# Reordering the end of the first attention step: transposes, copies on two engines, and a weight conversion in finer stages

## The chip, the cores and the metric

The kernel runs on one core of a Trainium2 chip. The metric is the device time of one execution in microseconds; the time before is 619.28 us, the median of three runs (618.98 to 620.67). The engines are named as in the profile: PE is TensorE (PEld its weight loads), DVE is VectorE, ACT is ScalarE, POOL is GpSimd, SP is SyncE, whose queue issues most of the transfers.

## What is computed

The reference is an attention block of the RWKV6 kind, followed by a gated feed-forward layer:

```
batch, n_heads, seq, head_dim = (4, 8, 768, 48)
for t in range(S):
    cur = np.einsum('bhd,bhe->bhde', u[None] * kt, vt)
    y[:, :, t] = np.einsum('bhd,bhde->bhe', rt, state + cur)
    state = wt[:, :, :, None] * state + np.einsum('bhd,bhe->bhde', kt, vt)
...
x = y as (B*S, H*D) = (3072, 384)
h = x @ w_in                       # 384 x 2048
sp = log(1 + exp(h))
out = (h * erf(sp)) @ w_out        # 2048 x 384
```

The two weight matrices arrive as float64; everything else is float32.

## The kernel before

**Steps.** The work is cut into 12 steps `s`. A step takes 128 positions of two batch entries with eight heads each, that is 256 rows of x. Six pairs of steps go through the sequence; steps 0 and 1 are the two halves of the batch at the first 128 positions, so they start from a state of zero. The order of instructions on every engine is written out by hand: inside `tc.manual_schedule` each engine runs its instructions in the order of the Python code, and what an instruction waits for follows from the tiles that it reads and writes.

**Attention of one step (`attend`, steps 0 to 4).** In-chunk products are built up over six levels. At each level TensorE multiplies r and k (`level_products`, L436) into a PSUM tile `pp`, VectorE multiplies half of r and k in place with products of the decays (`scale`, L252), and the products are taken over into `own` (L651 at level 1, a predicated copy at L448 for levels 2 to 5, ScalarE copies at L455 at level 6). Level 2 and later read what the scaling of the level below has written. The decay products `tot_sb` are made ahead on GpSimd (`prepare`, L304). After level 6 come:

1. `from_own(s, own, 1)`: half of own times v into the PSUM tile `y` (L470);
2. eight transposes of the scaled k into PSUM (L663) and the copy to `kT` on ScalarE (L667);
3. `state_part`: kT times v (L522), for both 64-position chunks `h`;
4. `from_own(s, own, 0)`: the other half;
5. `middle`, the state after the first chunk (two copies on VectorE, L692, in step 0), `faded` on GpSimd (L693), and the state for the next pair (`S_next`, L695);
6. `through_state`: r times the state into `y` (L496), then `y` is copied to SBUF as `xT` and `y3` (L503, L505, L506), and six small transfers bring rows of y3 into the free rows of xT (L510), three issued by SP and three by ScalarE.

`keep_busy` and `stay_warm` (L631) issue matmuls in step 0 and once in step 1 whose results nobody reads.

**Feed-forward.** `hidden` multiplies w_in with xT (L731), eight pieces of 12 matmuls a step, and `project` multiplies w_out with the gated result (L754). They run as pieces between the levels of later steps: `place(n)` is called after level n+1 and at the end, and issues conversion work (`convert_at`), activations and pieces. In step 1 one piece of step 0's hidden part runs at each place, so L731 waits for xT of step 0 and for the converted w_in.

**Conversion.** Each weight pair of slices (768 KB) is loaded as int32 words on SP (`load`, L194, three buffers `words`) and made float32 from its high and low words: ScalarE scales the high word into a PSUM tile (L207) and the low word into one of two `rest` buffers (L209); VectorE shifts (L216) and joins the sign (L219), writing w_in_sb or w_out_sb; GpSimd adds rest (L223). There are 16 such slices. `CONVERT[s][n]` lists what is issued at place n of step s: `l` a load, `s` both ScalarE operations, `j` the three operations that end a slice. Each letter keeps its own count. While slices are under way (`turns["converting"]`), the products of the attention use `pp0` alone, and the conversion uses `pp1`.

Of the kernel before, what the change touches and what calls it, by code (L numbers as in the profile page):

```python
# [11 lines left out]
FP32 = mybir.dt.float32  # L12
I32 = mybir.dt.int32
U32 = mybir.dt.uint32
AF = mybir.ActivationFunctionType
ALU = mybir.AluOpType

P = 128
EP = 64
HC = 64  # L20
NC = 2
NJ = 2
# [19 lines left out]
LOG = 6  # L42
# [18 lines left out]
def kernel(  # L61
# [14 lines left out]
    nc = tc.nc  # L76
# [51 lines left out]
    def products(shape):  # L128


        n = 0 if turns["converting"] else turns["next"]
        turns["next"] = 1 - n
        return ps_p.tile(shape, FP32, name=f"pp{n}")
# [46 lines left out]
    def convert(weights):  # L180

        held = {}

        def load(i):
            if i >= len(weights):
                return
            dst, src = weights[i]
            if src.dtype == FP32:  # L190
                nc.sync.dma_start(out=dst, in_=src)
                return
            words = wide.tile([P, 2, DM, 2], I32, name="words", bufs=3)
            nc.sync.dma_start(  # L194
                out=words[:].rearrange("p i n two -> p i (n two)"), in_=src.bitcast(I32)
            )
            held[i] = [words]

        def scale(i):
            if i in held:  # L200
                words = held[i][0]
                low, high = words[:, :, :, 0], words[:, :, :, 1]
                base = ps_p.tile([P, 2, NP * C], FP32, name="pp1")[:, :, :DM]
                rest = wide.tile([P, 2, DM], I32, name="rest", bufs=2)


                nc.scalar.mul(out=base, in_=high.bitcast(FP32), mul=2.0**-112)  # L207

                nc.scalar.mul(out=rest[:], in_=low.bitcast(U32), mul=2.0**-29)  # L209
                held[i] += [base.bitcast(I32), rest]  # L210

        def join(i):
            if i in held:
                words, bits, rest = held.pop(i)
                into = weights[i][0].bitcast(I32)
                nc.vector.tensor_scalar(  # L216
                    out=bits, in0=bits, scalar1=3, scalar2=None, op0=ALU.logical_shift_left
                )
                nc.vector.scalar_tensor_tensor(  # L219
                    out=into, in0=words[:, :, :, 1], scalar=-(1 << 31), in1=bits,  # L220
                    op0=ALU.bitwise_and, op1=ALU.bitwise_or,
                )
                nc.gpsimd.tensor_tensor(out=into, in0=into, in1=rest[:], op=ALU.add)  # L223

        done = {"l": 0, "s": 0, "j": 0}
        for _ in range(3):
            load(done["l"])
            done["l"] += 1
        while True:
            what = yield  # L230
            {"l": load, "s": scale, "j": join}[what](done[what])
            done[what] += 1
            if weights[0][1].dtype != FP32:
                turns["converting"] = 0 < done["s"] and done["j"] < len(weights)
                turns["next"] = 0

    def rows(e, n=D):
        return slice(e * EP, e * EP + n)
# [4 lines left out]

    ready = {}

    def scale(s, level):

        in_t, tots = loaded[s][0], ready[s][1]
        half, nb = 1 << (level - 1), JP * C >> level
        n = 1 if s > DIRECT and level == LOG else 2  # L250
        halves = view(in_t[:, 0:2], half, [[JP * C - half, n], [2 * half, nb], [1, half]])
        nc.vector.tensor_mul(  # L252
            halves, halves, view(tots[level - 1], 0, [[1, n], [2, nb], [0, half]])
        )

# [228 lines left out]
    def through_state(s, xT):  # L484

        c, in_t, _, _, S, _, _ = parts_of(s)
        for h, state in enumerate((S, middle)):
            if not (c or h):
                continue
            t = slice(h * HC, (h + 1) * HC)  # L490
            for j in range(NJ):
                for q in range(0, NP, 2):
                    for e in range(NE):
                        for p in (q + e, q + 1 - e):
                            n = j * NP + p
                            nc.tensor.matmul(  # L496
                                y[at(e, p), e, j, p // 2, t],
                                lhsT=state[rows(e), n, :], rhs=in_t[rows(e), 0, n, t],
                                start=False, stop=True, skip_group_check=True,
                            )  # L500

        y3 = att.tile([P, UNIT], FP32, name="y3", bufs=1)
        nc.scalar.copy(y3[:].rearrange("p (j t) -> p j t", j=NJ), y[:, 1, :, 1])  # L503
        for j in range(NJ):
            nc.scalar.copy(xT[:, 0:2, j * C : (j + 1) * C], y[:, 0, j])  # L505
        nc.scalar.copy(xT[:, 2, :].rearrange("p (j t) -> p j t", j=NJ), y[:, 1, :, 0])  # L506
        for kk in range(KT):
            n = D // KT
            for e, queue in enumerate((nc.sync, nc.scalar)):
                queue.dma_start(  # L510
                    out=xT[e * EP + D : (e + 1) * EP, kk, :],
                    in_=y3[e * EP + kk * n : e * EP + (kk + 1) * n, :],
                )

    def state_part(s, kT, ps):

        vt = loaded[s][1]
        for n in range(JP):
            for h in range(1 if s >= n_steps - SPC else NC):
                for e in range(NE):  # L520
                    t = slice(h * HC, (h + 1) * HC)
                    nc.tensor.matmul(  # L522
                        ps[h][rows(e), n, :D],
                        lhsT=kT[t, e * JP + n, :],
                        rhs=vt[t, n * NE + e, :],
                        start=True,
                        stop=True,
                    )

    def spread_blocks(s, pp):  # L530

# [78 lines left out]
    def attend(s, xT, place, behind):  # L610
# [14 lines left out]
                    rhs=zeros[:, :n], start=True, stop=True, skip_group_check=True,  # L625
                )

        def stay_warm(times=1, where=None):
            for _ in range(times):
                ps = where or ps_m.tile([P, NP * C], FP32, name="m")  # L630
                nc.tensor.matmul(  # L631
                    ps[:], lhsT=ident[:], rhs=ws[s][:, :NP], start=True, stop=True
                )
# [3 lines left out]
        for level in range(near_log(s) + 1 if s == DIRECT else 1, LOG + 1):  # L637
            rk = made[:] if level == 1 else RK
            pp = products([P, NE, JP, HC])
            level_products(pp, rk, level)  # L640
            if level == LOG and s == DIRECT:
                spread_blocks(s + 1, pp)
            scale(s, level)
            keep_busy(DM, DM // 2)
            if level == 1 and s == 1:
                stay_warm()
            got = pp[:].rearrange("p e n t -> p (e n) t")
            if level == 1:
                if not s:
                    nc.vector.tensor_copy(out=first[:], in_=mask_sb[:, 0, :])  # L650
                nc.vector.tensor_mul(  # L651
                    own[:], got, first[:, None, :].to_broadcast([P, NH, HC])
                )
            else:
                take_level(own, pp, level)
            if level > 1 and (s, level) != (DIRECT, LOG - 1):
                next(following, None)
            place(level - 1)

        from_own(s, own, 1)  # L660
        ps = products([P, JP, P])
        for n in range(JP):
            nc.tensor.transpose(ps[:, n, :], K[:, n, :], ident[:])  # L663
        if not s:
            stay_warm()
        kT = att.tile([P, NH, D], FP32, name="kT", bufs=1)
        nc.scalar.copy(  # L667
            kT[:].rearrange("p (e n) d -> p e n d", e=NE),
            ps[:].rearrange("p n (e d) -> p e n d", e=NE)[..., :D],
# [6 lines left out]
        place(LOG)  # L676


        if s:
            ps = products([P, NC, JP, HC])  # L680
            ps = [ps[:, h] for h in range(NC)]
        else:
            ps = [ps_m.tile([P, JP, HC], FP32, name="m") for h in range(NC)]
        state_part(s, kT, ps)
        from_own(s, own, 0)
        if not s:
            stay_warm(1, products([P, NP * C]))
        for e in range(NE):
            if c:
                nc.vector.tensor_add(middle[rows(e)], faded[0][rows(e)], ps[0][rows(e), :, :D])  # L690
# [105 lines left out]
    def in_order(s, k):  # L796
# [12 lines left out]


    CONVERT = (
        ("", "", "", "", "", "s", "jls", "j", "sl"),
        ("jsl", "jsl", "jsl", "jsl", "jsl", "j", "", "", "sl"),
        ("jsl", "jsl", "jsl", "jsl", "jsl", "js"),
        ("js", "j"),
    )
# [11 lines left out]
    with tc.manual_schedule(  # L828
# [20 lines left out]
        for s in range(n_steps):  # L849
# [3 lines left out]
            def convert_at(n):  # L853
                if s < len(CONVERT) and n < len(CONVERT[s]):
                    for what in CONVERT[s][n]:
                        conversion.send(what)
# [24 lines left out]
            if s > DIRECT:  # L881
                attend_late(s, place)
                continue
            attend(s, xTs[s], place, lambda: convert_at(LOG + 2))
            if s + 2 < n_steps:
                load_step(s + 2)
                if s + 2 == DIRECT:
# [107 lines left out]
```

## Time and profile before

| | |
|---|---|
| Median of 3 runs | 619.28 us (618.98 to 620.67) |
| Span of the profiled execution | 619.3 us |
| VectorE busy | 411.5 us, 459 instructions |
| ScalarE busy | 293.6 us, 374 instructions |
| GpSimd busy | 292.2 us, 295 instructions |
| Granted TensorE clock | 1.0 of full speed throughout |
| Moved by DMA | 63.27 MB, mean 102 GB/s |

In a line of the timeline the first number is the start in us from the beginning of the span, the second the duration, then engine, line, operation, what is written and read, the shape, and how many. A bracket at the end gives how long the engine had been idle before, and which engine's work ended that wait. L252 is line 252 of the kernel. The rows with PEld are weight loads that belong to the matmuls of the same line.

Step 0 ends near 31 us with L496, step 1 near 67 us, step 2 near 103 us. The last slice of w_in is converted by 61 us, w_out from 70 us on.

### The profile page before, as it was taken

To read this page: it belongs to the slowest core of one execution; us is meant where nothing else is said; L and a number is where in the kernel's file an instruction comes from. 1 tells how busy PE (TensorE), PEld (TensorE's weight loads), DVE (VectorE), ACT (ScalarE), POOL (GpSimd) and SP (SyncE) were. 2 spreads that over 40 slices of the span, in tenths; PEclk is the share of its full clock that TensorE was granted. 3 is DMA by queue.
4 is the path that set the end of the run, shared out by engine and by line. 5 is a ranking of instruction groups with operands and counts; after the bars stand their busy time and mean duration, and the time that the engine had idled before them with its cause. 6 is when DMAs were issued, how large, how long until landed. Compare 5 with 4: busy or idle time off the path is not lost.

```text
span 619.3 us, 15587 instructions
## 1 busy us (share of the span) xinstructions
PE 602.9 (97%) x6858; PEld 445.9 (72%) x6858; DVE 411.5 (66%) x459; ACT 293.6 (47%) x374; POOL 292.2 (47%) x295
## 2 busy tenths in 40 slices
PE   7889999999999999999999999999999999999997
PEld 6667787578668768668768768768668768668654
DVE  5697697894995897897697797797797321110300
ACT  2547878625536634443543543543443453634600
POOL 4448174601497389299199299299297000000000
PEclk9999999999999999999999999999999999999999
DMA  8375471440333405415415415405402100000000
GB/s 326 117 277 201 161 261 42 194 146 11 135 106 106 121 28 173 124 37 173 113 48 179 114 43 179 123 33 145 116 36 72 32 26 1 8 25 1 0 26 25
DMA packets 51371, 63.27 MB, mean 102 GB/s; under 512 B 34920, under 2 KB 40296, under 8 KB 49896
## 3 DMA queue, kind: packets, MB, share of 16 engines
q1 hardware_dynamic: 50152, 61.68, 31.1%
q8 instruction: 54, 0.88, 0.6%
q10 hardware_dynamic: 1152, 0.59, 0.4%
q14 instruction: 13, 0.11, 0.1%
HBM read 52.39 MB, written 8.69 MB: 99 GB/s over the span
## 4 chain that ended last, share of the span: by engine, by line
PE 83%; DVE 7%; issue 2%; POOL 2%; ACT 2%; DMA 2%; SPq 1%; DVEq 0%; POOLq 0%; ACTq 0%
PE m L731 37%; PE m L754 36%; PE pp L436 5%; DVE in L252 2%; PE y L470 2%; PE pp L522 1%; PE y L496 1%; DMA w<-in_rkw 1%; POOL tot_sb L304 1%; DMA in<-in_rkw 1%; PE pp L663 1%; DVE sums L356 1%; DVE pp L216 1%; DVE words L370 1%; DVE own L448 1%
## 5 line engine op out<-in xcount | busy, mean ns | idle before, releaser
L731 PE MATMUL m<-xT,w_in_sb 128*128 128x256 f32 x1152 | 257.2, 382 | 1.4 <-DVE w_in_sb L219 1.2
L754 PE MATMUL m<-w_out_sb,h 128*128 128x384 f32 x768 | 252.4, 488 | 1.3 <-POOL w_out_sb L223 1.3
L731 PEld LDWEIGHTS m<-xT,w_in_sb 128*128 128x128 f32 x1152 | 216.1, 190 | 33.7 <-issue 2.4
L754 PEld LDWEIGHTS m<-w_out_sb,h 128*128 128x128 f32 x768 | 144.5, 190 | 100.1 <-POOL w_out_sb L223 1.9
L740 ACT COPY h<-m 128x512 f32<-128x512 f32 x96 | 55.9, 582 | 128.3 <-PE m L731 128.2
L720 DVE TENSOR_TENSOR h<-h,sp 128x1024 f32<-128x1024 f32 x48 | 75.1, 1605 | 52.3 <-ACT sp L716 52.1
L252 DVE TENSOR_TENSOR in<-in,tot_sb 128x1024 f32<-128x1024 f32 (+1 forms) x60 | 86.1, 1443 | 29.3 <-PE pp L436 27.4
L370 POOL TENSOR_TENSOR words<-words,rest 128x528 f32<-128x528 f32 (+10 forms) x77 | 85.7, 1113 | 6.0
L366 POOL TENSOR_TENSOR rk<-words 128x528 f32<-128x528 f32 (+3 forms) x28 | 44.5, 1589 | 82.2 <-DVE sums L356 71.8
L763 ACT COPY o<-m 128x384 f32<-128x384 f32 x24 | 11.5, 480 | 112.2 <-PE m L754 112.2
L304 POOL TENSOR_TENSOR tot_sb<-tot_sb 128x256 f32<-128x256 f32 (+4 forms) x60 | 53.5, 892 | 4.5
L713 ACT ACTIVATE sp<-h 128x2048 f32<-128x2048 f32 x24 | 45.9, 1911 | 0.3
L716 ACT ACTIVATE sp<-sp 128x2048 f32<-128x2048 f32 x24 | 45.9, 1911 | 0.3
L436 PEld LDWEIGHTS pp<-in 48*64 48x64 f32 (+1 forms) x2368 | 33.8, 125 | 16.7 <-issue 10.4
L436 PE MATMUL pp<-in 48*64 48x64 f32 (+1 forms) x2368 | 38.4, 212 | 4.2 <-DVE in L252 1.5
L356 DVE TENSOR_REDUCE sums<-words 128x6 f32<-128x288 f32 (+8 forms) x66 | 29.2, 469 | 19.4 <-POOL words L366 19.2
L716 ACT ACT_TABLE_LOAD x24 | 30.8, 1283 | 16.3 <-issue 13.3
L366 POOL TENSOR_TENSOR words<-words 128x336 f32<-128x336 f32 (+6 forms) x49 | 35.1, 717 | 3.8
L356 DVE TENSOR_REDUCE sums<-rk 128x14 f32<-128x672 f32 (+9 forms) x54 | 34.8, 703 | 0.2
L713 ACT ACT_TABLE_LOAD x24 | 30.8, 1283 | 4.5 <-issue 4.1
L370 DVE TENSOR_TENSOR words<-words,rest 128x576 f32<-128x576 f32 (+8 forms) x34 | 27.9, 819 | 1.2
L223 POOL TENSOR_TENSOR w_out_sb<-w_out_sb,rest 128x768 int32<-128x768 int32 x8 | 17.8, 2229 | 18.3 <-DVE w_out_sb L219 18.3
(80 smaller groups left out, 438.0 us busy)
## 6 DMA issues: line engine op xcount, KB each, us to landing
in<-in_rkw SPq DMA_DIRECT2D x11, 1024.0 KB, 5.5
words<-in_moe_w_in SPq DMA_DIRECT2D x8, 768.0 KB, 4.4
words<-in_moe_w_out SPq DMA_DIRECT2D x8, 768.0 KB, 4.4
words<-in_rk_rows SPq DMA_DIRECT2D x8, 768.0 KB, 6.1
w<-in_rkw SPq DMA_DIRECT2D x11, 512.0 KB, 7.9
v<-in_v SPq DMA_DIRECT2D x12, 384.0 KB, 5.7
out<-o SPq DMA_DIRECT2D x24, 192.0 KB, 1.9
rest<-in_w_rows SPq DMA_DIRECT2D x8, 384.0 KB, 7.9
```

What stands on the lines that cost most here:

```text
L252: nc.vector.tensor_mul(halves, halves, view(tots[level - 1], 0, [[1, n], [2, nb], [0, half]]))
L304: nc.gpsimd.tensor_mul(new, pair[:, :, 0], pair[:, :, 1])
L356: nc.vector.tensor_reduce(out=view(sums[:], n, [[near * (NEAR + 1), NEAR // near], [NEAR + 1, near - n]]), in_=terms[n], axis=mybir.AxisLi ...
L366: engine.tensor_mul(terms[n], r[:, :, n:], k[:, :, : near - n])
L370: engine.tensor_mul(k[:, :, :m], k[:, :, :m], w[:, :, n : n + m])
L436: nc.tensor.matmul(pp[s0 : s0 + m, e, n, :m], lhsT=rk[rows(e), 1, n, s0 : s0 + m], rhs=rk[rows(e), 0, n, t0 : t0 + m], start=True, stop=True,)
L713: nc.scalar.activation(held[0][:], h[:], AF.Softplus)
L716: nc.scalar.activation(held[0][:], held[0][:], AF.Erf)
L720: nc.vector.tensor_mul(h[:, part], h[:, part], held[0][:, part])
L731: nc.tensor.matmul(ps[:, ff, :], lhsT=w_in_sb[:, g * FG + f + ff, kk * P : (kk + 1) * P], rhs=xT[:, kk, :], start=kk == 0, stop=kk == KT - 1,)
L740: nc.scalar.copy(h[:, f : f + FT, :], ps[:])
L754: nc.tensor.matmul(ps[j][:], lhsT=gs[g][:, f, j * C : (j + 1) * C], rhs=w_out_sb[:, g * FG + f, :], start=g + f == 0, stop=g == NG - 1 and ...
```

## The change

At the end of step 0 the transposes come first, into two PSUM tiles of the pool `ps_m`, and from_own after them; kT is copied in two halves, one by VectorE and one by ScalarE. A fence (a small VectorE copy out of y, L477 to L482) follows. The products of the state go chunk by chunk in step 0, into a tile `pp1`; middle is copied half by VectorE and half by ScalarE; GpSimd's faded follows at once, and the additions for S_next come after through_state. Two of the matmuls of stay_warm are gone, in step 0. In through_state the order of the matmuls runs over q from the last to the first, in all the steps that use it, and in step 0 the copies to xT (two of 256 columns) are VectorE's. The conversion has six stages instead of three (`l` load, `r` low word, `b` high word, `h` shift, `o` with_sign, `a` add); `s` now means r, then b, so that the low word comes ahead of the high word, and `j` means h, o, a. Slice 0 keeps its bits in `pp0`, slice 1 in two tiles of `ps_m`, with each of its VectorE and high-word operations in two halves. The scaling of level 1 in step 1 is GpSimd's, and `first` is made by ScalarE.

```diff
+        stages = {"l": load, "r": low_word, "b": high_word, "h": shift, "o": with_sign, "a": add}
...
+            for stage in {"s": "rb", "j": "hoa"}.get(what, what):
+                stages[stage](done[stage])
+                done[stage] += 1
...
-            for j in range(NJ):
-                for q in range(0, NP, 2):
+            for q in range(NP - 2, -1, -2):
+                for j in range(NJ):
...
-            nc.scalar.copy(xT[:, 0:2, j * C : (j + 1) * C], y[:, 0, j])
+            copy = nc.scalar.copy if s else nc.vector.tensor_copy
+            copy(xT[:, 0:2, j * C : (j + 1) * C], y[:, 0, j])
...
-            scale(s, level)
+            scale(s, level, nc.gpsimd if (s, level) == (1, 1) else None)
...
-                    nc.vector.tensor_copy(out=first[:], in_=mask_sb[:, 0, :])
+                    nc.scalar.copy(first[:], mask_sb[:, 0, :])
...
+        if not s:
+
+            half = JP // 2
+            turned = [ps_m.tile([P, half, P], FP32, name="m") for _ in range(2)]
+            for n in range(JP):
+                nc.tensor.transpose(turned[n // half][:, n % half, :], K[:, n, :], ident[:])
+            from_own(s, own, 1)
+            for x, copy in enumerate((nc.vector.tensor_copy, nc.scalar.copy)):
+                copy(
+                    kT[:].rearrange("p (e n) d -> p e n d", e=NE)[:, :, x * half : (x + 1) * half],
+                    turned[x][:].rearrange("p n (e d) -> p e n d", e=NE)[..., :D],
+                )
+            fence()
+            next(following, None)
+            place(LOG)
+            ps = ps_p.tile([P, NC, JP, HC], FP32, name="pp1")
+            ps = [ps[:, h] for h in range(NC)]
+            state_part(s, kT, ps)
+            from_own(s, own, 0)
+            for e, copy in enumerate((nc.vector.tensor_copy, nc.scalar.copy)):
+                copy(middle[rows(e)], ps[0][rows(e), :, :D])
+            nc.gpsimd.tensor_mul(faded[1][:], middle[:], ends[:, :, 1:2].to_broadcast([P, JP, D]))
+            for _ in following:
+                pass
+            place(LOG + 1)
+            through_state(s, xT)
+            behind()
+            for e in range(NE):
+                nc.vector.tensor_add(S_next[rows(e)], faded[1][rows(e)], ps[1][rows(e), :, :D])
+            behind(1)
+            return
...
     CONVERT = (
-        ("", "", "", "", "", "s", "jls", "j", "sl"),
-        ("jsl", "jsl", "jsl", "jsl", "jsl", "j", "", "", "sl"),
+        ("", "", "", "r", "r", "b", "h", "bola", "ho", "sl"),
+        ("ajsl", "jsl", "jsl", "jsl", "jsl", "j", "", "", "sl"),
```

## The prediction

> **What bounds the kernel now.** I read the page first (busy time, slices, chain), then the timeline of the first 60 us engine by engine, then the starts of steps 1 and 2, and last the gaps of TensorE.
>
> ```profile
> PE 602.9 (97%) x6858; PEld 445.9 (72%) x6858; DVE 411.5 (66%) x459; ACT 293.6 (47%) x374; POOL 292.2 (47%) x295
> PE   7889999999999999999999999999999999999997
> ```
>
> TensorE is the bound: 97% busy, and 83% of the chain that ended last is its own. So only its gaps, and matmuls that are fillers, can be won. The gaps between its matmuls sum to some 13 us; about 5 lie before 26 us, 1.23 us at 33.4, 1.25 us at 41.8, about 0.3 at 58.8, 0.9 at 66.8, two of 0.3 near 93 and 1.3 at 120.8. The change works on the stretch from 25.7 to 43. The timeline there, of before:
>
> ```profile
> 24.52 1.23 DVE L252 TENSOR_TENSOR in<-in,tot_sb 128x1024 f32<-128x1024 f32 x1 [0.28 <-PE pp L436]
> ...
> 27.50 0.80 ACT L667 COPY kT<-pp 128x768 f32<-128x768 f32 x1
> 28.36 0.81 PEld L522 LDWEIGHTS m<-v,kT 64*48 64x48 f32 x64 [0.96 <-ACT kT L667]
> ...
> 29.33 1.14 DVE L692 COPY middle<-m 48x384 f32<-48x384 f32 x2 [0.80 <-PE m L522]
> ...
> 30.73 0.66 PE L496 MATMUL y<-in,middle 48*48 48x64 f32 x32
> ...
> 32.41 1.86 SPq L510 DMA_DIRECT2D xT<-y  x3
> ...
> 34.61 3.31 PE L731 MATMUL m<-xT,w_in_sb 128*128 128x256 f32 x12 [1.23 <-DVE w_in_sb L219]
> ```
>
> It is a chain through four engines. The last scaling ends at 25.75, but kT is copied only at 27.50, because two conversions (25.67 and 26.57) stand before it on ScalarE; then come the state products, two copies of middle in a row, L496 (held to 30.73 by a filler that runs from 29.67 to 30.79), the copies to xT, their transfers, and L731. In step 1 a second thing limits:
>
> ```profile
> 38.79 1.82 POOL L223 TENSOR_TENSOR w_in_sb<-w_in_sb,rest 128x768 int32<-128x768 int32 x1 [1.45 <-DVE w_in_sb L219]
> ...
> 39.08 2.62 DVE L252 TENSOR_TENSOR in<-in,tot_sb 128x1024 f32<-128x1024 f32 x1 [0.43 <-PE pp L436]
> ...
> 43.04 1.16 PE L436 MATMUL pp<-in 48*64 48x64 f32 x64 [1.25 <-DVE own L448]
> ```
>
> The scaling of 1.22 us takes 2.62 because GpSimd's addition is running when it starts; it ends 1.1 us after that. From 43.04 on TensorE is nearly gapless to 58.4: what moves 43.04 moves the end.
>
> **What the Trainium skill says.** "SBUF — State Buffer", section "Who interferes with whom": VectorE with two SBUF inputs and a GpSimd operation that reads SBUF exclude each other for a whole instruction, and the first one in has it. The trace agrees: the row above, and the other way round at 44.88, where GpSimd's 1.82 us became 2.67. Operations with one input in PSUM are not held (L692 at its usual 0.57 each under an addition at 29.33). "GPSIMD Engine Reference", section 3.1: a two-input float operation there takes about twice VectorE's time, 4497 ns for 2048 elements. The trace has 1.04 us for 512 (L304). "DMA: Bandwidth & Descriptors", section "Queues, rings and completion order": an engine's transfers take their place in one ring per DMA engine and are consumed in ring order, SP's and ACT's in rings of their own. No pair in the trace so far shows a small transfer caught behind a large one at this place.
>
> **The change, part by part.**
>
> *Transposes first, kT shared.* They start at 25.80 and end at 26.89 (1.09 us for 8). from_own follows at 26.62 (next weight load 0.82 after the first, as now) and ends near 27.3. kT's ACT half lies between 0.37 (256 columns, L503) and 0.57 (512, L740), so 0.47: done 27.40 for 28.30 now; VectorE's half (0.57, from L692) lies before it. The two conversions that blocked ScalarE are split; the low words go to levels 4 and 5, where ScalarE is idle from 22.45 to 24.46 (twice 0.91 fits).
>
> *Fence, middle, scaling.* VectorE then has, in order from 27.35: fence 0.17 (later steps' L479), shift(0) 0.97, one half of middle 0.57, with_sign(0) 0.95, two xT copies. middle is whole at about 29.0 (30.47 now): the other half is ScalarE's, and both read only the first chunk's products, which now come first. Behind the fence wait the shift and middle, so it is charged. L496 runs 29.05 to 29.7 without the filler; two fillers (1.02 and 1.12 us) go.
>
> *xT.* The copies on VectorE, 256 columns from PSUM, are not in the trace: nothing under 0.28 (SBUF to SBUF, L277), 0.57 at most (384 columns). The page "VectorE: DVE Perf Modes", section on the errata, gives (120+256)/0.96 = 0.39 as an estimate; I take 0.42 each. They end at 30.7, so the xT transfers are issued at 30.7 for 32.41: 1.7 us earlier.
>
> *The load moves too.* load(3), 768 KB on SP, is issued when with_sign(0) ends, at 29.9 for 28.60, and now stands directly ahead of the xT rows on that queue. The DMA share of 28 to 34 us (0.15 us a digit) shows how long this one takes:
>
> ```profile
> DMA  0000000000990211979989989976000000000021
> ```
>
> From 1.0 us after its issue to 3.8 after: to 33.7. SP's xT rows, otherwise ready 1.25 us after issue (32.0), come behind it; with 0.4 us to be seen, L731 starts at 34.1 (34.61 now), but without its pauses between the three parts (2.86 us as at 38.94, for 3.31): it ends at 36.95 for 37.92, and level 2's products at 38.0 for 39.01. Bounds: no queueing, 37.1; a full extra microsecond, 39.0.
>
> *GpSimd's scaling.* 1024 elements: 2 x 1.04 = 2.1, or 2.25 from the page as an estimate; up to 3.5 if strides cost. GpSimd has faded to 29.9, add(0) to 31.8, the scaling to 34.0, add(1) to 35.9: before level 2 needs it at 36.95, so hidden. Behind it wait add(1) and add(2). Off VectorE come 1.22 us.
>
> *VectorE to level 2.* From 30.7: halves of shift(1) and with_sign(1) about 0.5 each (2.0), the state additions 1.11, own 1.13, shift(2) 1.0, with_sign(2) 0.95, starts spaced as in the trace: 36.9, for 38.65 now. add(2) then holds GpSimd from 36.95 to 38.8; level 2's products are done at 38.0, so VectorE's scaling waits again and ends at 39.8 for 41.70. **Gain here 1.9 us.**
>
> *Low words ahead of high words everywhere.* In steps 1 and 2 the low word fills a ScalarE wait for VectorE, if one of two rest buffers is free. At place 4 the previous additions end at 55.52 and 89.92, so both are through by 57.26 and 91.66 instead of 57.5 and 91.93: own's last level (L455) and L470 behind it come 0.25 us earlier, twice: **0.5 us**. But at the end of step 1 the high word is what VectorE waits for:
>
> ```profile
> 70.14 0.86 ACT L207 ACTIVATE pp<-words 128x768 f32<-128x768 f32 x1 [1.98 <-DVE own L651]
> ...
> 71.03 0.97 DVE L216 TENSOR_SCALAR pp<-pp 128x768 int32<-128x768 int32 x1 [0.92 <-ACT pp L207]
> ...
> 73.13 1.83 POOL L223 TENSOR_TENSOR w_out_sb<-w_out_sb,rest 128x768 int32<-128x768 int32 x1 [6.76 <-DVE w_out_sb L219]
> ...
> 74.55 1.49 DVE L252 TENSOR_TENSOR in<-in,tot_sb 128x1024 f32<-128x1024 f32 x1 [1.57 <-PE pp L436]
> ...
> 77.44 1.16 PE L436 MATMUL pp<-in 48*64 48x64 f32 x64 [0.17 <-DVE own L448]
> ```
>
> With 0.9 us of low word first, the addition runs from 73.95 to 75.8, the scaling of 74.55 ends at 76.9 for 76.04, and TensorE, now 0.17 us from gapless, loses **0.8 us**.
>
> *The rest.* first on ScalarE takes 0.38 off VectorE, but the next products end only 0.14 us before VectorE is done with own: 0.1. The order of through_state lets y3 be copied up to 0.15 us earlier; that counts where SP waits with step 4's load behind xT: 0.1. Sum: 1.9 + 0.5 + 0.2 - 0.8 = 1.8. The profiled span of 619.3 lies on the timed median of 619.28 (618.98 to 620.67), so **617.5**.
>
> **Rivals.** A, the sum above: 617.5, chance 0.60. B, the give-back at step 2 doesn't come, since VectorE or TensorE meets the addition in another phase there: 619.3 - 2.6 = 616.7, chance 0.20. For it: such collisions are a matter of tenths; against: both sides move together. C, the first stage keeps little, since the 768 KB ahead of xT and the addition in VectorE's way take a further 1.2 us: 618.7, chance 0.13. For it: two full-length instructions that the old order did not put there; against: both were priced. D, slower: the two rest buffers. Low word i must wait for addition i-2, and high word i now waits behind it. It decides where that addition ends later than 0.9 us before with_sign(i-1) does. By the trace at the third to fifth places it ends 0.8, 0.8 and 0.2 us before (47.55, 51.18, 55.52), so it costs 0.1 to 0.7 there, hidden by VectorE's own work. If it came through at ten places with 0.45 each, 4.5 us: 619.3 - 1.8 + 4.5 = 622.0, chance 0.07.
>
> **How the numbers follow.** 0.3% is 1.9 us, about what a measurement of this kernel tells from no change. A lies at that bound, so half of its 0.60 is faster, half not: faster 0.30 + 0.20 = 0.50, within 0.30 + 0.13 = 0.43, slower 0.07. The range takes in B and C with the bounds of queueing and GpSimd: 616.0 to 618.9; outside are D and the far ends.
>
> **What would show it.** kT near 27.4, L496 near 29, xT's transfers near 30.7, L731 near 34.1 without pauses, GpSimd's scaling 2.1 to 2.3 us, level 3 of step 1 near 41.1 (43.04), and in step 2 a gap before level 3. Wrong if level 3 of step 1 moves by less than 1 us, or if gaps open between 43 and 58.

## The result, and the profile after

The changed kernel takes 626.79 us (median; 624.79 to 627.23) against 619.22 us (618.98 to 620.67) for the kernel before on the same chip: a ratio of 1.0111, with a 95% interval of 1.0084 to 1.0138. The forecast was 617.5, with 616.0 to 618.9. The profiled execution has a span of 623.0 us for 619.3. Further down, one execution of e10 (1256 us) and one of the kernel before beside e9 to e12 (1597 us) took more than twice as long as the others and are in no ratio.

The page of the changed kernel, busy times and slices (compare the two PE lines shown of before, in whose profile the clock was 1.0 throughout):

```profile
PE 605.2 (97%) x6854; PEld 449.0 (72%) x6854; DVE 410.0 (66%) x462; ACT 293.1 (47%) x375; POOL 294.6 (47%) x296
PE   8889999999999999999999999999999999999997
PEclk9979999999999999999999999999999999999999
```

The profile lists each matmul of the code as two, so the two fillers less (matmuls whose results nobody reads) are four in its counts (6854 for 6858). With less to do, TensorE is yet busy 2.3 us longer. The reason is the 7 in the third slice of PEclk (31 to 47 us): the granted clock, the share of full speed at which the chip lets TensorE run, fell. The stages of the same stretch, in windows of 2 us (length; busy time and count of PE, PEld, DVE, ACT, POOL; then PE's clock, DMA share, GB/s), after:

```profile
32.00:34.00 2.00, 0.65 (x44) 0.51 (x34) 1.84 (x5) 0.49 (x2) 2.00 (x2) 1.00 0.84 295
34.00:36.00 2.00, 1.60 (x2) 0.30 (x2) 1.96 (x5) 0.15 (x1) 2.00 (x2) 0.66 0.32 106
36.00:38.00 2.00, 1.44 (x4) 1.06 (x4) 1.50 (x2) 1.77 (x3) 1.72 (x1) 0.50 0.56 106
38.00:40.00 2.00, 2.00 (x6) 1.55 (x6) 1.48 (x2) 1.11 (x2) 0.35 (x1) 0.50 1.00 411
40.00:42.00 2.00, 2.00 (x14) 1.40 (x16) 0.00 (x0) 0.45 (x2) 1.47 (x1) 0.63 1.01 426
```

and of before:

```profile
32.00:34.00 2.00, 1.38 (x26) 0.48 (x16) 1.93 (x3) 0.66 (x3) 0.00 (x0) 1.00 0.11 31
34.00:36.00 2.00, 1.37 (x5) 0.68 (x5) 2.00 (x3) 1.40 (x2) 1.34 (x1) 1.00 0.50 88
```

After has 0.65 us of matmuls in the first window where before has 1.38, and from 34.6 to 41.5 us its clock is half. The timeline of after, from level 6 of step 0 to level 3 of step 1:

```profile
24.22 0.74 PE L460 MATMUL pp<-in 48*32 48x32 f32 x64 [0.99 <-DVE own L472]
...
27.47 0.48 ACT L698 COPY kT<-m 128x384 f32<-128x384 f32 x1 [0.38 <-PE m L695]
...
27.85 1.34 PE L551 MATMUL pp<-v,kT 64*48 64x48 f32 x58
...
29.38 0.55 DVE L710 COPY middle<-pp 48x384 f32<-48x384 f32 x1 [0.23 <-PE pp L551]
...
30.01 0.47 ACT L710 COPY middle<-pp 48x384 f32<-48x384 f32 x1 [2.06 <-DVE middle L710]
...
32.16 0.76 DVE L530 COPY xT<-y 128x256 f32<-128x256 f32 x2 [1.37 <-ACT y L527]
...
32.99 2.75 SPq L535 DMA_DIRECT2D xT<-y  x3
...
33.13 2.81 POOL L276 TENSOR_TENSOR in<-in,w 128x1024 f32<-128x1024 f32 x1
...
34.40 1.82 PE L660 MATMUL m<-w,ident 128*128 128x512 f32 x2 [1.76 <-issue]
...
36.79 5.13 PE L785 MATMUL m<-xT,w_in_sb 128*128 128x256 f32 x12 [0.56 <-DMA xT<-y]
...
43.14 1.23 DVE L276 TENSOR_TENSOR in<-in,tot_sb 128x1024 f32<-128x1024 f32 x1 [3.63 <-PE pp L460]
...
45.74 1.16 PE L460 MATMUL pp<-in 48*64 48x64 f32 x64
```

The xT transfers are issued at 32.99, not 30.7 (before: 32.41). The first 12 hidden matmuls (L785; L731 before) start at 36.79 and take 5.13 us, where the pieces that follow take 2.86; the filler L660 takes 1.82 where before's took 1.13. Only the first of these two, 2.3 us, holds up what follows: the filler ends 0.56 us before xT is there. Level 3 of step 1 starts at 45.74, 2.7 us later than before. TensorE's last matmul then ends at 619.59 for 615.92, 3.7 later; most of the rest comes in step 2, as predicted:

```profile
77.01 2.31 DVE L276 TENSOR_TENSOR in<-in,tot_sb 128x1024 f32<-128x1024 f32 x1 [0.78 <-PE pp L460]
...
80.68 1.04 PE L460 MATMUL pp<-in 48*64 48x64 f32 x55 [0.95 <-DVE own L472]
```

The idle time ahead of this level 3 was 0.17 us before and is 0.95 now.

The theory taken to the chip was: half clock, because TensorE has too little to do while it waits for xT, with the fillers gone (called T1 below). The main rival (T2): what holds level 3 back is the schedule itself (GpSimd's scaling, the order of the words, the load ahead of xT), and the clock costs little.

### The profile page after: what moved, and what is told of

It is laid out like the page before. It is cut to its first block, busy times and chain, and to the rows that moved or that the text cites. A ratio compares the mean times of both kernels' runs of the same rounds, so it can differ in the third digit from the quotient of the medians.

```text
span 623.0 us, 15586 instructions
## 1 busy us (share of the span) xinstructions
PE 605.2 (97%) x6854; PEld 449.0 (72%) x6854; DVE 410.0 (66%) x462; ACT 293.1 (47%) x375; POOL 294.6 (47%) x296
## 4 chain that ended last, share of the span: by engine, by line
PE 80%; DVE 7%; POOL 5%; DMA 3%; ACT 2%; issue 2%; SPq 0%; DVEq 0%; POOLq 0%; ACTq 0%
PE m L808 35%; PE m L785 34%; PE pp L460 4%; POOL tot_sb L328 2%; DVE in L276 2%; PE y L494 2%; PE pp L551 2%; PE y L520 1%; POOL w_out_sb L245 1%; PE m L887 1%; POOL w_in_sb L245 1%; DMA in<-in_rkw 1%; DMA w<-in_rkw 1%; DVE own L472 1%; DVE sums L380 1%
## 5 line engine op out<-in xcount | busy, mean ns | idle before, releaser
L785 PE MATMUL m<-xT,w_in_sb 128*128 128x256 f32 x1152 | 259.0, 384 | 0.7 <-DMA xT<-y 0.6
L785 PEld LDWEIGHTS m<-xT,w_in_sb 128*128 128x128 f32 x1152 | 218.0, 191 | 33.8 <-POOL in L276 2.1
```

Of the source, the lines that this page charges most:

```text
L785: nc.tensor.matmul(ps[:, ff, :], lhsT=w_in_sb[:, g * FG + f + ff, kk * P : (kk + 1) * P], rhs=xT[:, kk, :], start=kk == 0, stop=kk == KT - 1,)
```

## The experiments

No kernel here leaves out or changes a part of the computation; some add or drop fillers. Ratios are to the kernel before on the same chip, with 95% intervals. e1 to e4 ran together, and so did e5 to e8, e9 to e12 and e13 to e16; the kernel before took 620.55, 620.85, 620.94 and 620.63 us beside them.

**e1: two fillers put back.** Two matmuls of 512 columns behind through_state of step 0, into the tile of the state products:

```diff
             through_state(s, xT)
+            for _ in range(2):
+                nc.tensor.matmul(
+                    ps[0].rearrange("p n t -> p (n t)"), lhsT=ident[:], rhs=ws[s][:, :NP],
+                    start=True, stop=True, skip_group_check=True,
+                )
             behind()
```

> The changed kernel with two filler matmuls (512 columns each, into the half of the state's PSUM tile that is already read) put behind through_state of step 0. Theory T1, the granted clock: the changed kernel ran from 34.6 to 41.5 us at half clock because TensorE had too little to do from 30 to 36 us; with the fillers the clock stays at 1.0, the first 12 matmuls of L785 take 2.9 to 3.3 us instead of 5.13, and level 3 of step 1 starts near 43.7 instead of 45.74: 2 to 4 us off the changed kernel (about 621 to 624 us in the timed runs, against 626.8). Rival T2, that the loss comes from the serial copies, the load ahead of xT and the order of the conversions: no gain, or 1 us lost to the fillers.

Measured: 621.97 us, ratio 1.0026 (1.0014 to 1.0038). TensorE in e1, level 1 of step 1 to level 3 (the rows are shown from the new matmuls on, L717):

```profile
31.81 1.98 PE L717 MATMUL pp<-w,ident 128*128 128x512 f32 x4
33.73 1.16 PE L460 MATMUL pp<-rk 48*64 48x64 f32 x64
34.82 1.13 PE L660 MATMUL m<-w,ident 128*128 128x512 f32 x2
37.00 2.83 PE L790 MATMUL m<-xT,w_in_sb 128*128 128x256 f32 x12 [1.06 <-DMA xT<-y]
39.76 1.16 PE L460 MATMUL pp<-in 48*64 48x64 f32 x64
40.85 2.86 PE L790 MATMUL m<-xT,w_in_sb 128*128 128x256 f32 x12
44.08 1.16 PE L460 MATMUL pp<-in 48*64 48x64 f32 x64 [0.37 <-DVE own L472]
```

The hidden matmuls start 0.2 us later than in the changed kernel and end 2.1 us earlier. Work that nobody reads makes the kernel faster. A loss of 1.0 us at level 3 stays (44.08 for 43.04), which the clock, at 1.0 here, doesn't explain.

**e2: the kernel before without its two step-0 calls of stay_warm.** Is their absence enough?

```diff
-        if not s:
-            stay_warm()
...
-        if not s:
-            stay_warm(1, products([P, NP * C]))
```

> The kernel before without the two fillers in step 0 (the third, in step 1, stays). T1: the same dip of the granted clock appears in the old order, between about 30 and 42 us, and the time grows by 2 to 5 us to 621 to 624. T2: the fillers were only in the way of L496 (0.26 us); the time stays or falls by up to 0.3 us, with the clock at 1.0.

Measured: 620.41 us, ratio 1.0007 (0.9991 to 1.0022); the clock stays at 1.0. T1's expectation failed. The windows of e2:

```profile
32.00:34.00 2.00, 1.18 (x9) 0.30 (x2) 1.94 (x3) 0.44 (x2) 0.00 (x0) 1.00 0.11 31
34.00:36.00 2.00, 1.55 (x5) 0.84 (x6) 2.00 (x3) 1.43 (x2) 1.32 (x1) 1.00 0.49 85
```

and its first hidden matmuls:

```profile
34.43 3.32 PE L727 MATMUL m<-xT,w_in_sb 128*128 128x256 f32 x12 [1.25 <-DMA xT<-y]
```

With 1.18 us of work in the first window and a wait of 1.25 us ahead of the hidden matmuls it holds. So the lost fillers alone, in the old order, cost nothing that can be told from noise. The changed kernel adds longer waits: L660 alone is preceded by 1.76 us of idle time. The row names no releaser; by the code its `ps_m` tile is one that slice 1's bits occupied, and VectorE's with_sign for their first half (L237, two from 33.76 for 1.01 us) ends just ahead of it.

**e3: high word ahead of low word again.**

```diff
-            for stage in {"s": "rb", "j": "hoa"}.get(what, what):
+            for stage in {"s": "br", "j": "hoa"}.get(what, what):
...
-                held[i].append(rest)
+                held[i].insert(1, rest)
```

> The changed kernel with the high word ahead of the low word again in every 's'. By the prediction's step on the end of step 1: the gap of 0.95 us before level 3 of step 2 (79.73 in the changed kernel) goes, 0.8 us gained, and 0.5 us lost at own's last level in steps 1 and 2: 0.3 us net. T1 leaves the clock's dip as it is. If the reordering is what makes the kernel slower, it gains 2 us or more.

Measured: 626.05 us, ratio 1.0077 (1.0049 to 1.0105). The scaling ahead of level 3 of step 2 takes 1.50 us again instead of 2.31, and the wait there is gone; two gaps of 0.3 us near 98 us return. Both halves of the prediction's term are seen, but the clock is half from 35 to 45 us, so the order of the words isn't what brings it down.

**e4: the scaling of level 1 in step 1 back on VectorE.**

```diff
-            scale(s, level, nc.gpsimd if (s, level) == (1, 1) else None)
+            scale(s, level)
```

> The changed kernel with the scaling of level 1 in step 1 on VectorE again. If GpSimd's scaling (2.81 us at 33.13) holds up the additions and with them L785, the first matmuls of L785 start earlier than 36.79 and 1 to 2 us come back. By T1 it is hidden: L785 waits for xT (36.7), the time changes by less than 0.7 us, and VectorE's own chain (own, shift, with_sign) comes about 1.2 us later.

Measured: 625.35 us, ratio 1.0064 (1.0041 to 1.0087), and half clock all the same. In the profile the hidden matmuls start at 36.78, as in the changed kernel, and stop for 1.84 us after four. GpSimd's scaling is not what brings the clock down. The half clock lasts 3.4 us in this profile, and the intervals of this ratio and of the changed kernel's overlap, so whether the edit gains a little is not told.

**e5: the filler of step 1 moved.** One filler behind through_state as in e1, and the one at level 1 of step 1 (L660) dropped: does it matter where the work lies, or only how much there is?

```diff
-            if level == 1 and s == 1:
-                stay_warm()
```

> The changed kernel with as many fillers as it has, but the one of step 1 (which waits from 32.65 to 34.40 us for a PSUM buffer that slice 1's bits hold) put ahead of it, directly behind through_state, into a tile that is free. Theory T1b: what lets the clock fall is not the number of fillers but the stretch from 32.6 to 34.4 us in which TensorE stands still for that buffer; with the filler ahead of level 1's products the stretch is cut, the clock stays at 1.0 in most runs and 2 to 4 us come back. Rival T1a, that two fillers' work is missing: the dip stays, since TensorE then has nothing at all from about 33.5 to 36.8 us.

Measured: 625.19 us, ratio 1.0063 (1.0043 to 1.0084). TensorE in e5:

```profile
32.62 1.16 PE L460 MATMUL pp<-rk 48*64 48x64 f32 x64
37.32 5.36 PE L788 MATMUL m<-xT,w_in_sb 128*128 128x256 f32 x12 [3.54 <-DMA xT<-y]
```

One stretch of 3.54 us without work, and half speed, which starts at 35.6, 1.8 us into it. The theory behind this run (T1b: a filler ahead of level 1's products is enough) failed: the same count of fillers elsewhere does not hold the clock.

**e6: e1, with the order of the state products of before, and the tiles' turns repaired.** In the changed kernel each new letter of CONVERT sets the turn of the product tiles to zero, also ahead of the conversion. Level 6 of step 0 thus gets the tile that level 5's copy still reads: it starts at 24.22, with the wait for L472 in the row shown of after (before: 23.66).

```diff
-                turns["next"] = 0
+                if turns["converting"]:
+                    turns["next"] = 0
...
-            if s
+            if True
             else ((n, h) for h in chunks for n in range(JP))
```

> The kernel with the two fillers behind through_state (clock at 1.0, level 3 of step 1 at 44.08, level 6 of step 0 at 24.38 us), and in it two things as before: the stage letters no longer reset the turn of the two product tiles, so that level 6 goes to the other tile than level 5, and the state's products run over both chunks in the old order. If these are what shifts the early stretch, level 6 starts near 23.7 (0.6 us earlier), the 64 products of the state take 0.94 us for about 1.4, and level 3 of step 1 comes 0.8 to 1.0 us earlier. If not, the time stays.

Measured: 623.4 us, ratio 1.0039 (1.0025 to 1.0052). The two repairs do what they were made for: level 6 starts at 23.68, the 64 state products take 0.90 us, and level 3 of step 1 starts at 42.78, 1.3 us before e1's. But the end is no earlier. The repair of the turns also changes which tile stands next when the conversion is over, and this opens a wait in step 3:

```profile
116.93 0.29 PE L461 MATMUL pp<-in 48*64 48x64 f32 x4 [1.28 <-DVE w_out_sb L237]
```

**e7: e1, with load(3) behind xT's transfers.**

```diff
-        ("", "", "", "r", "r", "b", "h", "bola", "ho", "sl"),
+        ("", "", "", "r", "r", "b", "h", "boa", "lho", "sl"),
```

> The kernel with the two fillers behind through_state, and in it the load of slice 3 issued behind the xT transfers in place of ahead of them. If the 768 KB hold up xT, the first 12 matmuls of L785 then start 2.2 us after the transfers' issue (35.4 in place of 37.0) and end near 38.7 for 39.8; level 3 gains up to 1 us, less where VectorE's scaling then waits for GpSimd's addition. If xT isn't held up by it, nothing moves.

Measured: 622.19 us, ratio 1.0026 (1.0014 to 1.0038), as e1. The transfers in e1:

```profile
33.16 2.73 SPq L535 DMA_DIRECT2D xT<-y  x3
33.17 2.72 ACTq L535 DMA_DIRECT2D xT<-y  x3
```

and the rows of e7:

```profile
33.55 1.86 SPq L535 DMA_DIRECT2D xT<-y  x3
...
36.17 3.01 PE L790 MATMUL m<-xT,w_in_sb 128*128 128x256 f32 x12
...
39.71 1.82 POOL L245 TENSOR_TENSOR w_in_sb<-w_in_sb,rest 128x768 int32<-128x768 int32 x1 [1.84 <-DVE w_in_sb L237]
...
40.40 2.22 DVE L276 TENSOR_TENSOR in<-in,tot_sb 128x1024 f32<-128x1024 f32 x1 [0.83 <-PE pp L460]
```

From the issue of xT's transfers to the first hidden matmul it is 2.6 us, where e1 needs 3.8 (33.16 to 37.00). So the 768 KB ahead of xT cost at least 1.2 us (in e7 TensorE has no wait ahead of L790, so xT may have been there sooner). By the landing times of the traces, SP's transfers land 3.1 us after their issue in e1 and 1.8 in e7 and before. ScalarE's three, on a queue of its own without a load, land 3.6 us after it in e1 (2.1 before): they are the last, so a place behind the load in SP's queue is not what sets the end. Level 2 comes 0.65 us earlier (39.11 for 39.76), but its scaling now meets GpSimd's addition, takes 2.22 us, and level 3 starts at 44.00 (e1: 44.08). A gain of 0.65 us is used up by one collision.

**e8: fillers and all five repairs** (the fillers of e1; e3, the two repairs of e6, e7, and the xT copies of step 0 all on ScalarE):

```diff
-            copy = nc.scalar.copy if s else nc.vector.tensor_copy
+            copy = nc.scalar.copy
```

> All of these in one: two fillers behind through_state, the turns and the order of the state's products as before, slice 3's load behind xT, the high word ahead of the low word, and all of xT's copies on ScalarE. By the sums: from the kernel with fillers (span 620.3) 0.9 for turns and order, up to 1 for the load, 0.6 for the high word, 0.3 for the hand-overs between engines: 617.5 to 618.5, that is 1 to 2 us faster than the kernel before. If the clock dips again in some runs, a spread of 3 us and more.

Measured: 621.91 us, ratio 1.0002 (0.9986 to 1.0019): not the 1 to 2 us under before that were expected. Level 3 of step 1 starts at 41.34, 1.7 us earlier than before and near the 41.1 that the prediction had named. By level 6 of step 1 half of it is gone (53.80 for 54.68), behind a conversion that starts late:

```profile
48.47 0.88 ACT L218 ACTIVATE pp<-words 128x768 f32<-128x768 f32 x1 [3.15 <-DVE own L473]
...
49.14 1.05 PE L461 MATMUL pp<-in 48*64 48x64 f32 x56
```

The row names VectorE's L473, which ends at 48.43. But the load of these words was issued at 43.10 and takes 5.4 us to land, to 48.5, while the DMA engines are busy throughout (386 GB/s from 43 to 50 us). So I read this as the load setting the pace here; the two ends lie too close to be told apart, and no run here tests it. The wait of step 3 seen in e6 is 2.13 us in this run, and after it the clock is half for 3.4 us.

**e9: e8 with the turns repaired another way**, so that only the early low words leave them alone:

```diff
-                turns["next"] = 0
+                if what != "r":
+                    turns["next"] = 0
```

> The kernel with all the corrections (fillers, order of the state's products, slice 3's load behind xT, high word first, xT's copies on ScalarE), but now only the letter r leaves the turn of the product tiles alone. In its predecessor level 3 of step 3 got the tile that slice 15's bits held, waited 2.13 us for with_sign, and the clock then fell for 3.4 us. If that was the turn, this gap goes and the clock stays: span near 617.5, 0.2% faster than the kernel before in undisturbed runs, whose spans are 617 to 619. What caps the gain: slice 5's words arrive only at 48.4 us, whatever is done earlier, so 0.9 of the 1.7 us won at level 3 of step 1 remain. If the gap at 115 us stays, it is GpSimd's wait for step 4's decays instead.

Measured: 620.16 us, ratio 0.9990 (0.9976 to 1.0004), where 0.2% under before was expected. The wait in step 3 is gone; the clock of this profile is half for 3.4 us elsewhere, from 255 us.

**e10: the changed kernel with one filler instead of e1's two.**

```diff
+            for _ in range(1):
```

> The changed kernel with one filler more behind through_state, where two held the clock. A dose for theory T1: with TensorE busy some 1 us less between 31 and 36 us than with two, the clock falls in some executions and not in others: mean clock between 0.994 and 1.0, time between that with two fillers (622) and the changed kernel (626.8). If only the sum of work counts and one suffices, it is as with two; if two were needed in full, it is at 626.

Measured: 623.13 us, ratio 1.0045 (1.0021 to 1.0069): between none and two. This run shows best what goes with the clock, since kernel and chip are the same. Of its other eleven executions four have a mean granted clock of 1.0 and take 621.7 us in the mean; four have 0.997 and take 623.1; three have 0.992 and take 627.0. A mean of 0.992 over 627 us is half clock for 10 us, which loses 5.0 us of work; the difference to full clock is 5.3. The mean doesn't say where the clock fell. In the one profile, at 0.997, it was not here but from 16.4 to 19.9 us, behind a wait of 1.21 us in step 0. The profile of before has the same stretch there, with a wait of 1.22 us, and kept the clock.

**e11: e9 without any filler of its own, and e12: with three.**

```diff
-            for _ in range(2):
+            for _ in range(3):
```

> The corrected kernel without the two fillers behind through_state. All the earlier waits are shortened, the turns, the load, the state's products and the copies are right. If those were the cause of the slow clock (TensorE waiting too long), the clock holds and the time is 619 or below. By T1 TensorE has too little work from 29 to 34 us even so: dips in some or all runs, 1 to 3 us slower than with fillers.

> The corrected kernel with three fillers in place of two. If two already hold the clock and the third lies in time in which TensorE waits for xT anyway, the same time as with two, within 0.1%; if it pushes level 1's products and L785 back, 0.5 to 1 us slower; if two leave dips in some executions, a smaller spread.

Measured: e11 620.64 us, 0.9997 (0.9977 to 1.0017); e12 619.9 us, **0.9983 (0.9973 to 0.9994)**, the only version whose interval lies below 1. It overlaps that of e9, so the third filler is not told from two here. In e11's profile the clock falls at 32.0 for 3.4 us:

```profile
30.00:32.00 2.00, 1.60 (x93) 1.50 (x82) 1.85 (x5) 1.77 (x6) 2.00 (x2) 1.00 0.03 8
32.00:34.00 2.00, 1.70 (x3) 0.24 (x3) 1.95 (x4) 0.21 (x1) 2.00 (x2) 0.51 0.12 33
```

Its filler at level 1 of step 1 and the first hidden matmuls:

```profile
31.74 1.76 PE L661 MATMUL m<-w,ident 128*128 128x512 f32 x2 [0.40 <-PE pp L461]
33.80 3.64 PE L786 MATMUL m<-xT,w_in_sb 128*128 128x256 f32 x12 [0.30 <-DMA xT<-y]
```

It fell although TensorE had 1.60 us of matmuls in the two microseconds before and no wait over 0.54 us (ahead of L521, at 29.29); e2 kept it with 1.18 us and a wait of 1.25. So neither the work in two microseconds nor the longest wait tells by itself when it falls. What it costs here is little: level 3 still starts at 41.27, and the repairs without any filler take back the whole loss of the changed kernel, as far as the interval tells. TensorE in e12:

```profile
30.18 2.84 PE L718 MATMUL pp<-w,ident 128*128 128x512 f32 x6
32.95 1.16 PE L461 MATMUL pp<-rk 48*64 48x64 f32 x64
34.04 1.12 PE L661 MATMUL m<-w,ident 128*128 128x512 f32 x2
35.00 2.75 PE L791 MATMUL m<-xT,w_in_sb 128*128 128x256 f32 x12
...
41.80 1.16 PE L461 MATMUL pp<-in 48*64 48x64 f32 x64 [0.16 <-DVE own L473]
```

No wait from 30.2 to 41.6 us. Its TensorE ends at 614.48, 1.4 us ahead of before.

**e13 to e16: how much is the clock's?** e13 is the changed kernel again, e14 repeats e1, e15 has three fillers, e16 is e14 with e3's order of words, all on one chip.

> The changed kernel as it is, beside its versions with fillers on the same chip. Clock theory: half clock after 34 us again, mean clock below 0.998 in most executions, and a ratio of 1.006 to 1.011, with level 3 of step 1 near 45.7 us. The rival, that the schedule alone makes the loss and the chip the difference between the earlier runs, gives a ratio within 0.2% of that of e14.

> Changed kernel with two filler matmuls behind through_state of step 0 (the same as e1). Clock theory: clock 1.0 there, level 3 of step 1 near 44.1 us, ratio about 1.0026 as in e1, so 0.4 to 0.8% under e13. Rival: the same ratio as e13.

> With three fillers. If two already keep the clock in every execution, the same ratio as e14 or up to 0.1% more, since a third filler (about 1 us) ends before xT is there; if some executions with two still fall to half clock, 0.1% less than e14.

> As e14, but with the high word ahead of the low word in the coarse letter s, as in the kernel before. The prediction's give-back: 0.8 us at level 3 of step 2 goes, and 0.5 us of gaps near 98 us comes back, so 0.3 us or 0.05% under e14. If the order of the words does not matter to the end, the same ratio within 0.1%.

| kernel | median | ratio to before | profiled span | level 3 of step 1 |
|---|---|---|---|---|
| before | 620.63 us | 1 | | |
| e13, no filler | 627.49 us | 1.0102 (1.0074 to 1.0131) | 625.5 us | 48.49 |
| e14, two | 622.63 us | 1.0036 (1.0022 to 1.0051) | 620.2 us | 44.34 |
| e15, three | 621.8 us | 1.0021 (1.0009 to 1.0032) | 620.3 us | 44.22 |
| e16, two, high word first | 622.41 us | 1.0030 (1.0018 to 1.0043) | 619.8 us | 43.84 |

TensorE in e13:

```profile
34.61 1.10 PE L660 MATMUL m<-w,ident 128*128 128x512 f32 x2 [1.76 <-issue]
37.32 2.04 PE L785 MATMUL m<-xT,w_in_sb 128*128 128x256 f32 x4 [1.61 <-DVE own L680]
40.03 3.75 PE L785 MATMUL m<-xT,w_in_sb 128*128 128x256 f32 x8 [0.67 <-issue]
43.71 1.99 PE L460 MATMUL pp<-in 48*64 48x64 f32 x64
```

Two fillers take 0.66% off, three 0.81%, of a loss of 1.02%. As the fillers only add work, I put what they take off down to the clock: between two thirds and four fifths of the loss. e10's executions agree: at full clock they lie 1.2 us over those of before at full clock beside them (621.7 for 620.5), where e13's median is 6.9 over. In e13 the half clock lasts longer than in the first profile and reaches the products of level 2 (1.99 us for 1.16), which is part of why its level 3 is later. The profile of e14 has half clock too, but ahead of all this, from 16.2 to 19.6 us as in e10, so its 44.34 is not free of it. Between e14 and e16 the order of the words makes 0.06%; the intervals overlap, so that much is not told from none, though the collision is gone (the scaling of step 2 takes 1.49 us again). What stays with three fillers is 0.21%, or 1.3 us. In the profile of e15 it is 1.2 us at level 3 of step 1 and 0.8 in step 2, less 0.3 us for one gap fewer near 94; of this sum of 1.7, 1.0 is left at TensorE's last matmul (616.88 for 615.92).

## Why the prediction was wrong

**The step that failed** is the clause "two fillers (1.02 and 1.12 us) go" under "Fence, middle, scaling", with the reading that opens the prediction, that fillers are matmuls that can be won. I counted a filler only as something in the way of L496, and nothing for what it keeps up. What the runs showed in its place: half clock for 6.8 and 10.2 us in the two profiles of the changed kernel, and two fillers put back take 0.66% off. The clock was 1.0 throughout in the profile of before, so that trace showed no price; the other bound of this unknown had to be put, and it was not. The price is not paid for the fillers alone: without them the old order lost nothing (e2), and neither did the repaired one (e11, 0.9997). It was paid in an order in which xT came later too, and the terms of that follow below. No rival held it either: D, the one slower case, put its 4.5 us into the two rest buffers. The Trainium skill, "TensorE: Matmul & The Clock Gate", section "Part 1: The HAM clock gate (the "warmup" mystery)", says that TensorE falls to half its clock after an idle window of about 3.4 us, and that these windows run freely. The runs agree on the step and the unit: half clock, for 3.4 us (e8, e9, e11), 6.8 us (after) or 10.2 us (e13). They go beyond it on the trigger: no wait in the first profile of the changed kernel was over 1.76 us in this stretch, and in e11 none was over 0.54 ahead of the fall. That one and the same stretch near 16 us kept the clock in the profile of before and lost it in e10's fits with windows that run freely, but no run here tests it. How little work is too little is not settled.

**Why TensorE waited longer.** Three terms of the sum were mis-sized, all on the way to xT (issued at 32.99, predicted 30.7), and a wait was not foreseen:

- "Transposes first, kT shared" had kT at 27.40; it was 27.95. The first 0.56 us are the turn of the tiles at level 6, which the step did not look at (e6 takes it back).
- "middle is whole at about 29.0": it was 30.48. Most of it has two causes. The fence, and the shift behind it, started at 28.10 for 27.35, since from_own came later; VectorE was busy with the shift until 29.15. And ScalarE's half of the copy waited for VectorE's half, though they read different partitions: 0.6 us. A further 0.23 us is a wait of VectorE for the products. They go chunk by chunk now, so that a whole chunk of them works on the same 64 rows of TensorE's array (their row group), where before the rows changed every two matmuls; with from_own among them they last from 27.85 to 29.33 instead of 0.90 us (e6). The page named above, section "Part 3: Packing small matmuls — row/col tiling", says that a weight load overlaps a running matmul only when the row group differs; e6 against after agrees, though from_own no longer runs among the products there.
- "xT": the two copies took 0.76 us, near the estimate of 0.84, but the hand-overs from ScalarE to VectorE and back raise the time from y3 to the transfers to 1.24 us. Before and e12 have all on ScalarE and need 0.95.
- Not foreseen: L660 waits 1.76 us, by the code for a tile of `ps_m` that slice 1's bits hold. The step that puts the bits there was costed on VectorE alone.

**"The load moves too"** was right that the 768 KB delay xT. From the issue of the transfers to the first hidden matmul it had 3.4 us (30.7 to 34.1) for the 2.2 of before; it was 3.8 (32.99 to 36.79), so the size was 0.4 us short, within its bound. (It read the end of the load off the DMA row of before as 3.8 us after its issue; the row ends at 3.6.) The reason it gave does not explain the end: the order in SP's ring, which it drew from the Trainium skill's "DMA: Bandwidth & Descriptors", section "Queues, rings and completion order", fits SP's transfers (3.1 us to land for 1.8), but ScalarE's, in rings of their own, land last (3.6 us). By which way the load slows those is open.

**"GpSimd's scaling"** was 2.81 us for 2.1 to 2.25, within the bound of 3.5. In e4, without it, the hidden matmuls start no earlier (36.78), so it is hidden behind xT as predicted.

**"Low words ahead of high words everywhere"** was right in both signs: 0.95 us of wait at level 3 of step 2 (0.8 predicted over the 0.17 there) and one gap fewer at own's last level in step 2, 0.3 of the 0.5 predicted. e14 and e16 don't tell its effect on the end from none.

**"VectorE to level 2"**, the 1.9 us, did not appear in the changed kernel; with repairs and fillers it is 1.7 (e8) or 1.2 us (e12). So the gain was there to be had, but half of e8's is gone again by level 6. Of the signs put, level 3 of step 1 moved, but 2.7 us the wrong way; no gap opened between 43 and 58. Of the rivals, none happened as put. D would go with the order of the words, and e16, which takes that order back, is not told from e14.

That the clock made most of the loss is shown by e13 to e15 and by the executions of e10. That missing fillers alone don't cost this much is shown by e2 and e11. What exactly lets the clock fall is open: in e11 it fell without a long wait. Which of the repairs makes e12 faster than before was not taken apart.

## What to carry to other kernels

Before a filler matmul is taken out, or a wait of TensorE is made longer, put a price on it that takes in a slower clock, even where the trace at hand shows none: here half clock came for 3.4 to 10.2 us at a time, which costs half as much. Look at several executions, since the same kernel kept its clock in some and lost it in others. When a stage is reordered, follow each tile's buffer to its last reader: here most of the mis-sized terms were tiles that two engines or two stages shared, not durations. And a gain at one point is only kept as far as the next resource allows: one collision between VectorE and GpSimd took all of it in e7, and a late conversion half of it in e8.

## What the runs showed of the hardware

- The clock at half speed makes twelve matmuls of 2.86 us take 5.13 and 5.36. It came in stretches of 3.4, 6.8 and 10.2 us. With more work it fell less often here: both profiles of the changed kernel show it here (after and e13), and its mean clock was 0.988 to 0.995 in all ten executions; with one filler it was 0.992 to 1.0; with two or three, repairs or not, none of nine profiles shows it at this place, though some show it at others. The kernel before is not free of it either: its 54 executions beside e13 to e16 have 0.994 to 1.0.
- Small transfers beside a load of 768 KB landed 3.1 us after their issue where they stood behind it on its queue, and 3.6 us on another engine's queue (e1); without it 1.8 and 2.1 us (before).
- ScalarE's copy of 48 partitions out of a PSUM tile began when VectorE's copy of 48 other partitions of that tile had ended (30.01 after 29.38 + 0.55), in e12 as well (29.07 after 28.44 + 0.54). So the shared copy took 1.10 us, where the two in a row on VectorE took 1.14 before. Whether the hardware or the tile's bookkeeping orders them was not tried.
- The strided in-place scaling takes 2.81 to 2.83 us on GpSimd and 1.22 on VectorE.
